# DeltaNet attention with a top-1 MoE on one core: the inverses' steps handed out by estimated VectorE time, norms and v moved later, blocks 12 to 15 routed as four

## The chip, the cores and the metric

One Trainium2 chip, of which one core is used. The metric is the device time of one execution in microseconds (us). The engines are TensorE (PE; its weight loads are listed apart as PEld), VectorE (DVE), ScalarE (ACT), GpSimd (POOL) and SyncE (SP), whose queue issues nearly all of the DMAs. Each engine works through its own queue in the order in which the program wrote it.

## The reference

Two layers. The first is a delta-rule recurrence over 768 tokens for 4 batches x 8 heads with head size 48; the second sends every one of the 3072 tokens (384 wide) to the one of 8 experts that its gate picks.

```python
# q, k, v: (4, 8, 768, 48); beta: (4, 8, 768); w1: (8, 384, 1024); w2: (8, 1024, 384)
k_n = k / (norm(k) + 1e-6)
for t in range(S):
    y[t] = q[t] @ state
    v_old = state^T k_n[t]
    state = state + beta[t] * outer(k_n[t], v[t] - v_old)
x = y as (3072, 384)
expert = argmax(x @ w_gate); gate = softmax value of that expert
out[token] = gate * (relu(x[token] @ w1[expert]) @ w2[expert])
```

## The kernel before, in words

**Blocks and steps.** The tokens are cut into 6 spans of 128 (`tb` from 0 to 5); a span of one batch with its 8 heads is a block, so there are 24 blocks, n = 4 tb + b. Inside a block the recurrence is solved in chunks of 32 tokens (`q` from 0 to 3) with the inverse of a triangular 32 x 32 matrix for each chunk and head. The main loop runs over steps t from 0 to 26. Step t works at once on chunk q of block t - q, for the four q's, in four groups of 32 partitions, so a block passes through four steps and a new one comes in at each.

**One step.** `residual(t)` (lines 441 to 470): TensorE adds up in `ks` what the state and the earlier chunks give, and VectorE subtracts it from v (line 470). `apply(t)` (473 to 485): TensorE multiplies the result with the inverses `wt` (line 478), ScalarE copies it to `u` (line 483). Line 478 can't start before line 470 has ended. Between the two, TensorE has the previous block's output transposes (`emit_x`, line 548, 8 matmuls) and in steps 1 to 4 a handful of filler matmuls (line 691, table `WD`). Then `finish(t - 3)` gives the outputs of the block that is complete, and `qpart` and `kpart` make the products for later blocks. At seven places of a step (`beside(t, i)`, i from 0 to 6) other work is written into the queues: entries of the list `off` that are due, steps of the inverses, steps of the routing (`fine`), pieces of the expert weights and of expert 0's first tokens (from step 20 on).

**The inverses.** Each span's inverses are made on VectorE alone, for all 32 (batch, head) pairs and 4 chunks at once. `prepare(tb)` computes the norms of k and scales the products (lines 320 to 362). `lanes(tb)` is the inverse: 16 columns, each with a multiplication (line 374) and a subtraction (line 385) on the two 16 x 16 halves, then `combine` for the lower left quarter (multiplications of line 395, additions of line 403), then one transpose into `wt` (line 418). That is 53 steps of the generator, of very different length. Span 0 is done ahead of the loop. Span tb is done in the steps 4 (tb - 1) to 4 tb - 1, and its transpose not before step 4 tb - 1. What is not yet done when step 4 tb begins is written there in one go. How many generator steps a place may take is a fixed count: `STEPS` (`STEPS0` in the first four steps); `prepare` uses the same count and gets three more of its own steps at each place.

**The mask.** `mask()` (line 303) is a GpSimd pass over the products that `qpart` left. It is made to wait for the last VectorE instruction that was noted ahead of the step ("beside the residual").

**Norms and v.** `norms` transposes the norms on VectorE (line 351) and writes them with four small DMAs of SP's queue into `nt_all` (line 354). `scale_v` (line 428) multiplies v with them, two steps' worth at once, in the odd steps; span tb's norms are first used in step 4 tb - 1. `load_v(tb, i)` loads chunk i of span tb's v into a ring of 8 (line 180) right behind `apply(t)` at t = 4 (tb - 1) + i - 1.

**Routing.** A finished block's rows go through `emit_x` into a row buffer, and `emit_slots` (lines 578 to 677) gives each token a slot in its expert's list: five small VectorE instructions (lines 589 to 606), counting matmuls (559), `pos` (625), `sli` (650), and one scatter per block from GpSimd's queue (658). Blocks 0 to 11 do this in fours, 12 to 15 in pairs, 16 on one by one. A set that has been started stands in the list `fine`; only its first member goes on. With fours, the scatters of the first pair are written one step after the set's start and those of the second pair one step later. The row buffers of blocks from 12 to 21 are two tiles of two rows, by turns; single blocks use half of one.

**Experts.** From step 20 on weights are loaded and split; expert 0's first tokens run in steps 23 to 26, and behind the loop the experts follow each other on TensorE.

Of the kernel before, what the change touches and what calls it, by code (L numbers as in the profile page):

```python
# [8 lines left out]
F32 = mybir.dt.float32  # L9
# [9 lines left out]
B, H, S, D = 4, 8, 768, 48  # L19
C = 128  # L20
NT = S // C
NB = C // 32
# [9 lines left out]
NN = NT * B  # L32
# [4 lines left out]
ROW = DM + E + 2  # L37
# [5 lines left out]
def deltanet_moe(ctx, tc, qT, kT, kr, v, beta, w_gate, w1, w2, out):  # L43
    nc = tc.nc
# [58 lines left out]
    HB = 16  # L103
# [1 line left out]
    LAG = NB - 1  # L105
    FILL = (0, 1, 4, 5, 6, 7, 2, 3)

    STEPS = (3, 3, 3, 3, 2, 2, 2)

    STEPS0 = (3, 3, 2, 2, 2, 2, 2)  # L110
    FINE = (3, 3, 3, 2, 2, 2, 2)
    W0 = 42
    WD = {1: 12, 2: 15, 3: 14, 4: 3}
    W1 = 8
    W4 = 12
    DM2 = 0
    DEF = 2
    AH = 3
# [12 lines left out]
    rp = ctx.enter_context(tc.tile_pool(name="rp", bufs=1, side="left"))  # L131
    lp_ = ctx.enter_context(ExitStack())
    ep_ = ctx.enter_context(ExitStack())
    lp = lp_.enter_context(tc.tile_pool(name="lp", bufs=1, side="left"))
    fp = ep_.enter_context(tc.tile_pool(name="fp", bufs=1, side="right"))
# [21 lines left out]
    nt_t = lp.tile([128, (NT * B + LAG) * H], F32, name="nt_all")  # L157
# [9 lines left out]
    tiles = {tb: {b: {} for b in range(B)} for tb in range(NT)}  # L167
# [150 lines left out]
    def prepare(tb):  # L318

        T = tiles[tb]  # L320
        if tb == 0:
            T["lg"] = fp.tile([128, LW], F32, name="lg0", tag="lg", bufs=2)
            tiles["mark"] = nc.vector.transpose(out=full(T["lg"]), in_=tiles["dg"]).ins
            yield
        lg = T["lg"]
        lw = T["lw"]
        ss, s0, r0 = (lp.tile([128, 32], F32, name=f"{n_}{tb}", tag=n_) for n_ in ("ss", "s0", "r0"))
        nc.vector.tensor_scalar(out=ss, in0=lg[:, 0:1024:33], scalar1=1e-36, scalar2=None, op0=ALU.max)
        for _ in range(6 if tb > 1 else 1):
            yield  # L330
        nc.scalar.activation(out=s0, in_=ss, func=AF.Sqrt)
        yield
        nc.vector.reciprocal(r0, s0)
        yield
        nc.vector.tensor_tensor(out=r0, in0=r0, in1=ss, op=ALU.mult)
        yield
        nc.vector.tensor_tensor(out=s0, in0=s0, in1=r0, op=ALU.add)
        yield
        nc.vector.tensor_scalar(out=s0, in0=s0, scalar1=0.5, scalar2=1e-6, op0=ALU.mult, op1=ALU.add)
        yield  # L340
        nc.vector.reciprocal(r0, s0)
        yield
        nc.vector.tensor_tensor(out=ss, in0=r0, in1=bl[:, tb, :], op=ALU.mult)
        yield
        nc.vector.tensor_tensor(out=lw.rearrange("p a b -> p (a b)")[:, 0:1024:33], in0=ss, in1=r0, op=ALU.mult)
        yield
        nc.vector.tensor_tensor(out=r0, in0=ss, in1=r0, op=ALU.mult)
        yield
        def norms():
            sn = lp.tile([128, 32], F32, name=f"sn{tb}", tag="sn")  # L350
            nc.vector.transpose(out=sn, in_=s0)
            for q in range(NB):
                p = slice(32 * q, 32 * q + 32)
                nc.sync.dma_start(out=nt_t[p, (B * tb + q) * H:(B * tb + q) * H + 32], in_=sn[p])
            yield

        nc.vector.tensor_tensor(out=blocks(lg), in0=blocks(lg), in1=r0.rearrange("p (f r) -> p f r", f=2).unsqueeze(3)
                                .broadcast_to([128, 2, HB, HB]), op=ALU.mult)
        T["scaled"] = True
        yield  # L360
        yield from norms()
        T["nt"] = True

    def lanes(tb):


        T = tiles[tb]
        lg, lw = full(T["lg"]), T["lw"]

        def product(nm, rows, cols, c):  # L370
            m, w = rows.stop - rows.start, cols.stop - cols.start
            x = fp.tile([128, 256 if rows.stop > 16 and c < 16 else 64], F32, name=f"{nm}{tb}_{c}", tag=nm, bufs=2)
            x = x[:, 0:m * w].rearrange("p (a b) -> p a b", a=m)
            noted(nc.vector.tensor_tensor(out=x, in0=lg[:, rows, c:c + 1].broadcast_to([128, m, w]),  # L374
                                          in1=lw[:, c:c + 1, cols].broadcast_to([128, m, w]), op=ALU.mult))
            return lw[:, rows, cols], x

        for c in range(HB):
            todo = [product("ta", slice(c + 1, 32), slice(0, c + 1), c)]
            if c < HB - 1:  # L380
                k = HB + c
                todo.append(product("tb", slice(k + 1, 32), slice(HB, k + 1), k))
            yield
            for y, x in todo:
                tiles["mark"] = noted(nc.vector.tensor_tensor(out=y, in0=y, in1=x, op=ALU.subtract))  # L385
            yield

        def combine(g):

            n, r0 = 4 * g + 4, HB + 4 * g  # L390
            x = fp.tile([128, 1024], F32, name=f"tc{tb}_{g}", tag="tc", bufs=2)
            x = x[:, 0:64 * n].rearrange("p (a j b) -> p a j b", a=4, j=n)
            for a0, a1 in ((0, 2), (2, 4)) if n > 8 else ((0, 4),):
                m = a1 - a0
                noted(nc.vector.tensor_tensor(out=x[:, a0:a1], in0=lw[:, r0 + a0:r0 + a1, HB:HB + n].unsqueeze(3)
                                              .broadcast_to([128, m, n, HB]),
                                              in1=lw[:, HB:HB + n, 0:HB].unsqueeze(1).broadcast_to([128, m, n, HB]),
                                              op=ALU.mult))
                yield
            while n > 1:  # L400
                h, k = n // 2, n - n // 2
                y = x[:, :, 0:h] if n > 2 else lw[:, r0:r0 + 4, 0:HB].unsqueeze(2)
                tiles["mark"] = noted(nc.vector.tensor_tensor(out=y, in0=x[:, :, 0:h], in1=x[:, :, k:n], op=ALU.add))
                n = k
                yield

        pair = [combine(g) for g in range(3, -1, -1)]
        while pair:
            for x in pair[0:2]:
                if next(x, 0) == 0:  # L410
                    pair.remove(x)
                else:
                    yield

        T["cols"] = True
        yield
        T["wt"] = lp.tile([128, BH, 32], F32, name=f"wt{tb}", tag="wt", bufs=2)
        tiles["mark"] = noted(nc.vector.transpose(out=T["wt"].rearrange("p h t -> p t h"), in_=lw))
        if tb + 2 < NT:
            clear_w(tb + 2)  # L420
        yield

    def scale_v(t):

# [62 lines left out]
    def finish(n):  # L487

        tb, b = n // B, n % B
# [5 lines left out]
        for p in range(NP):  # L495
            for a in range(2):
                x = slice(64 * (a ^ p % 2), 64 * (a ^ p % 2) + 64)
# [18 lines left out]
        for h in range(H):  # L516
            p, r = h // 2, 64 * (h % 2 ^ h // 2 % 2)
# [7 lines left out]
        j, m = n % w, min(w, 2)  # L525
# [1 line left out]
            tiles["rows"] = []  # L527
            tiles["rl"] = lp.tile([128, w, E], F32, name=f"rl{tb}_{b}", tag=f"rl{w}", bufs=2)
        if j % m == 0:
            pool, tag = (fp, "rowb") if j >= 2 else (rp, "row") if n < NN - 2 else (xq_[0], "row")  # L530
            t = pool.tile([128, 2 if n < NN - 2 else 1, ROW], F32, name=f"row{tb}_{b}", tag=tag, bufs=2)
            tiles["rows"].append(t[:, 0:m])
        xp = emit_x(n, yt, tiles["rows"][-1][:, j % m])
        yield
# [137 lines left out]
    def run(gen, steps=1):  # L672

        for _ in range(steps):
            if next(gen, tiles) is tiles:
                return False
        return True
# [283 lines left out]
    before = [(tb, prepare(tb)) for tb in range(1, NT)]  # L961
    W = None

    def inverses(steps, t, i=0):

        while steps > 0 and queue:
            tb, lane = queue[0]
            if t < B * (tb - 1) and "cols" not in tiles[tb - 1] or ("cols" in tiles[tb] and t < B * tb - 1):
                break
            if before and before[0][0] == tb:  # L970
                if (t, i) < READY.get(tb, (0, 0)):
                    break
                if run(before[0][1]):
                    steps -= 1
                else:
                    before.pop(0)
            elif run(lane):
                steps -= 1
            else:
                queue.pop(0)  # L980

    ahead, other = early(), rest()
    order = list(EO)
# [5 lines left out]
    def beside(t, i):  # L989

        tiles["t"], tiles["at"] = t, i
        due(t, i)
        inverses((STEPS0 if t < B else STEPS)[i], t, i)
        if before and (t, i) >= READY.get(before[0][0], (B * before[0][0] - B, 0)):
            if not run(before[0][1], 3):
                before.pop(0)
        for _ in range(FINE[i] if t < NN - B else 4):
            if fine and not run(fine[0]):
                fine.pop(0)
        for _ in range(WSL.count((t, i))):  # L1000
            run(W)
        for _ in range(ES.count((t, i))):
            ahead_step()

    fin = iter(())
    for t in range(NN + LAG):
# [31 lines left out]
        run(copies, 2)  # L1038
        for tb in range(1, NT):
            for i in range(NB):  # L1040
                if t == max(B * (tb - 1) + i - 1, 0):
                    load_v(tb, i)
        beside(t, 2)
        fin = finish(t - LAG) if t >= LAG else iter(())
# [280 lines left out]
```

## Time and profile before

| | us |
|---|---|
| median of 3 runs | 518.15 |
| the three runs | 517.04, 518.15, 521.36 |
| the profiled execution | 522.53 |
| its span, first to last instruction | 520.7 |
| TensorE busy | 484.5 |
| VectorE busy | 337.7 |
| ScalarE busy | 254.7 |
| GpSimd busy | 112.8 |

A stretch of the trace is given in us from the span's start. The steps of the loop take from 36 us to 284 us; the experts follow. "Idle before" is the time in which an engine did nothing before an instruction, with the instruction that ended the wait; "issue" stands for a wait that no semaphore of the trace explains. The granted clock is a share of TensorE's full speed: 1.00 is 2.4 GHz and 0.50 is 1.2 GHz; a value between them is a mean over a stretch with both.

### The profile page before, as it was taken

The page shows a single profiled execution, that of the slowest core. Times are in us where ns is not written, and L with a number is a line of the kernel's source. Part 1 is how long each engine was busy: PE and PEld are TensorE (multiplying, and loading weights), DVE is VectorE, ACT ScalarE, POOL GpSimd, SP SyncE. Part 2 cuts the span into 40 slices and gives each one's busy share as a digit, 9 for nine tenths or more (in the row PEclk, how much of TensorE's full clock was granted, in tenths as well). Part 3 has the DMA queues.
Part 4 walks back from the last instruction along what each step waited for, and adds up shares of the span by engine and source line. Part 5 has one row for each costly group of instructions (what it writes and reads, how often), then busy time and mean ns, then how long its engine had stood idle before and what let it go on. Part 6 is the DMA issues. An engine that isn't in the chain of part 4 may idle for free.

```text
span 520.7 us, 17340 instructions
## 1 busy us (share of the span) xinstructions
PE 484.5 (93%) x7286; PEld 434.8 (83%) x7291; DVE 337.7 (65%) x975; ACT 254.7 (49%) x539; POOL 112.8 (22%) x148
## 2 busy tenths in 40 slices
PE   7699899998998979999999999999999999999991
PEld 5656678887887868777889999999999999999991
DVE  2989959898689998465322976465756646565310
ACT  3413556674675645775343564444436444444210
POOL 6010121242242333323122001203030210303121
PEclk9999999997999989997999999999999999999997
DMA  6589747757554443762041595473847547481000
GB/s 197 121 194 256 188 140 192 220 157 183 145 156 107 136 121 107 244 198 91 18 102 68 163 239 157 121 183 115 203 124 164 160 134 161 141 197 36 13 18 27
DMA packets 74844, 74.14 MB, mean 142 GB/s; under 512 B 46649, under 2 KB 62506, under 8 KB 74764
## 3 DMA queue, kind: packets, MB, share of 16 engines
q1 hardware_dynamic: 71308, 63.45, 46.5%
q0 software_dynamic: 3456, 9.57, 5.1%
q8 instruction: 58, 0.95, 0.8%
q14 instruction: 22, 0.18, 0.1%
HBM read 54.25 MB, written 19.42 MB: 141 GB/s over the span
## 4 chain that ended last, share of the span: by engine, by line
PE 50%; issue 1%; ACT 1%; DMA 1%; SPq 1%; DVE 1%; POOL 1%; ACTq 0%; POOLq 0%
PE h L813 21%; PE y L824 18%; PE y L1131 4%; PE xp L548 1%; PE yp L518 1%; DMA w1r<-in_w_dram 1%; SPq L737 1%; PE ks L451 1%; PE ks L478 1%; PE pq L284 1%; PE ks L463 1%; PE xt L889 0%; POOL out_dram L827 0%; PE yp L498 0%; ACT pm L296 0%
## 5 line engine op out<-in xcount | busy, mean ns | idle before, releaser
L824 PE MATMUL y<-w2h,hx 128*128 128x384 f32 x352 | 93.2, 339 | 0.4 <-DVE hx L817 0.4
L827 POOL DMA_INDIRECT out_dram<-yo,idx x32 | 40.3, 1259 | 197.5 <-ACT yo L1126 113.0
L824 PEld LDWEIGHTS y<-w2h,hx 128*128 128x128 f32 x352 | 64.0, 188 | 1.2 <-DVE hx L817 1.1
L483 ACT COPY u<-ks 32x384 f32<-32x384 f32 x96 | 45.1, 469 | 33.7 <-PE ks L478 23.6
L813 PE MATMUL h<-xh,w1l 128*128 128x448 f32 x168 | 61.3, 365 | 0.0
L813 PE MATMUL h<-xh,w1h 128*128 128x448 f32 x168 | 61.2, 365 | 0.0
L813 PE MATMUL h<-xl,w1h 128*128 128x448 f32 x168 | 61.1, 363 | 0.0
L824 PE MATMUL y<-w2l,hx 128*128 128x384 f32 x176 | 59.4, 337 | 0.0
L698 DVE TENSOR_TENSOR w2l<-w2r,w2h 128x768 fp32r<-128x768 f32 x32 | 30.6, 957 | 40.6 <-ACT w2h L697 40.0
L817 DVE SCALAR_TENSOR_TENSOR hx<-h,hx 128x448 fp32r<-128x448 f32 (+1 forms) x64 | 37.5, 587 | 29.8 <-ACT hx L816 29.2
L816 ACT ACTIVATE hx<-h 128x448 fp32r<-128x448 f32 (+1 forms) x64 | 33.2, 518 | 44.8 <-PE h L813 44.8
L303 POOL TENSOR_SCALAR_AFFINE_SELECT pm<-pm 128x1024 f32<-128x1024 f32 x24 | 26.3, 1095 | 91.0 <-DVE tb L374 24.9
L1126 ACT ACTIVATE yo<-y,gt 128x384 f32<-128x384 f32 x22 | 12.8, 582 | 64.5 <-PE y L824 36.6
L451 PE MATMUL ks<-st,kt 112*32 112x96 f32 x768 | 43.5, 253 | 0.7 <-ACT st L512 0.5
L451 PEld LDWEIGHTS ks<-st,kt 112*32 112x32 f32 x768 | 32.4, 111 | 5.5 <-issue 1.9
L385 DVE TENSOR_TENSOR lw<-lw,ta 128x31 f32<-128x31 f32 (+7 forms) x96 | 36.6, 381 | 0.2
L284 PE MATMUL pg<-kt 48*128 48x128 f32 x384 | 31.7, 317 | 5.2 <-DMA kt<-in_kT_dram 4.2
L698 DVE TENSOR_TENSOR w1l<-w1r,w1h 128x1024 fp32r<-128x1024 f32 x24 | 29.4, 1225 | 9.0 <-ACT w1h L697 8.6
L478 PE MATMUL ks<-v_all,wt 32*32 32x48 f32 x1536 | 25.8, 206 | 10.1 <-DVE v_all L470 6.6
L284 PEld LDWEIGHTS pg<-kt 48*128 48x128 f32 x384 | 28.3, 222 | 8.3 <-issue 5.2
L658 POOL DMA_INDIRECT xg<-row,sli x22 | 22.6, 1028 | 58.0 <-ACT yt L522 20.4
L478 PEld LDWEIGHTS ks<-v_all,wt 32*32 32x32 f32 x1536 | 21.4, 107 | 16.4 <-DVE v_all L470 9.8
(166 smaller groups left out, 1038.3 us busy)
## 6 DMA issues: line engine op xcount, KB each, us to landing
w1r<-in_w_dram SPq DMA_DIRECT2D x24, 512.0 KB
w2r<-in_w_dram SPq DMA_DIRECT2D x32, 384.0 KB
xg<-zrow SPq DMA_DIRECT2D x14, 394.0 KB
kt<-in_kT_dram SPq DMA_DIRECT2D x24, 224.0 KB
qt<-in_qT_dram SPq DMA_DIRECT2D x24, 224.0 KB
xr<-xg SPq DMA_DIRECT2D x28, 168.0 KB
ku<-in_kr_dram SPq DMA_DIRECT2D x20, 192.0 KB
v_all<-in_v_dram SPq DMA_DIRECT2D x15, 192.0 KB
```

The source lines that it names most:

```text
L284: ins = nc.tensor.matmul(pg[a][:, p], lhsT=kt[r, p], rhs=xt[r, p], start=True, stop=True, tile_position=(64 * a, 0), skip_group_check=True)
L303: ins = nc.gpsimd.affine_select(out=pm, in_=pm, compare_op=ALU.is_gt, fill=0.0, base=0, pattern=[[0, H], [1, C]], channel_multiplier=-1)
L385: tiles["mark"] = noted(nc.vector.tensor_tensor(out=y, in0=y, in1=x, op=ALU.subtract))
L451: nc.tensor.matmul(ks[32 * q:32 * q + 32, 2 * p:2 * p + 2, :], lhsT=kt_t[n % KTL][0:RP, p, 32 * q:32 * q + 32], rhs=st_view(n % B, p), sta ...
L478: ins = nc.tensor.matmul(ks[r, h, :], lhsT=tiles[n // B]["wt"][r, n % B * H + h, :], rhs=vn[r, h, :], start=True, stop=True, tile_position ...
L483: nc.scalar.copy(out=uview(n)[r], in_=ks[r])
L698: nc.vector.tensor_tensor(out=lo, in0=src, in1=hi.bitcast(F32), op=ALU.subtract)
L813: nc.tensor.matmul(ps, lhsT=w[:, d, fs], rhs=x_[:, d], start=(n == 0), stop=(n == len(terms) - 1))
L816: nc.scalar.activation(out=hh, in_=ps, func=AF.Relu)
L817: nc.vector.scalar_tensor_tensor(out=hl, in0=ps, scalar=0.0, in1=hh.bitcast(F32), op0=ALU.max, op1=ALU.subtract)
L824: nc.tensor.matmul(ps, lhsT=h(f)[h_], rhs=w2[w][:, f, :], start=(n == 0), stop=(n == len(terms) - 1))
L827: nc.gpsimd.indirect_dma_start(out=out, out_offset=bass.IndirectOffsetOnAxis(ap=idx, axis=0), in_=yo, in_offset=None, bounds_check=N - 1, ...
```

## The change

Four edits.

1. **Shares.** A generator step of `lanes` now hands out an estimate of its VectorE time, `cost(n)` = 0.105 + 0.00098 n us for each instruction on n elements, and 1.92 for the transpose. A place of a step takes generator steps until its share (`SHARE`, 1.1 us at the first four places, 0.73 at the last three) is used up; what it went over is taken off at the next place. A step of `prepare` counts 0.3.
2. **Norms.** From span 2 on the four DMAs of the norms are put into `off` and written at step 4 (tb - 1) + 1, place 2.
3. **v.** From span 2 on `load_v(tb, i)` is written one step later, at t = 4 (tb - 1) + i.
4. **Blocks 12 to 15.** `W4` is 16, so they choose slots as one four. Their second row buffer is in another pool (one tile of two rows), and the single blocks 16 to 21 have two one-row tiles of their own (`rowc`).

```diff
-    STEPS = (3, 3, 3, 3, 2, 2, 2)
-    STEPS0 = (3, 3, 2, 2, 2, 2, 2)
+    SHARE = (1.1, 1.1, 1.1, 1.1, 0.73, 0.73, 0.73)
+    PREP = 0.3
-    W4 = 12
+    W4 = 16
...
+            if tb < 2:
+                spread()
+            else:
+                off.append(((B * (tb - 1) + 1, 2), spread))
+                off.sort(key=lambda x: x[0])
...
+    def cost(n):
+        return 0.105 + 0.00098 * n
...
         for c in range(HB):
             todo = [product("ta", slice(c + 1, 32), slice(0, c + 1), c)]
...
-            yield
-            for y, x in todo:
+            c_ = sum(x[2] for x in todo)
+            yield c_
+            for y, x, _ in todo:
                 tiles["mark"] = noted(nc.vector.tensor_tensor(out=y, in0=y, in1=x, op=ALU.subtract))
-            yield
+            yield c_
...
-        yield
+        yield cost(1850)
...
-            pool, tag = (fp, "rowb") if j >= 2 else (rp, "row") if n < NN - 2 else (xq_[0], "row")
-            t = pool.tile([128, 2 if n < NN - 2 else 1, ROW], F32, name=f"row{tb}_{b}", tag=tag, bufs=2)
+            pool, tag, k = ((fp if n < 12 else lp, "rowb", 2) if j >= 2 else (rp, "row", 2) if n < 16 else
+                            (lp, "rowc", 1) if n < NN - DEF else (xq_[0], "row", 1))
+            t = pool.tile([128, k, ROW], F32, name=f"row{tb}_{b}", tag=tag, bufs=1 if pool is lp and k > 1 else 2)
...
-    def inverses(steps, t, i=0):
-        while steps > 0 and queue:
+    def inverses(share, t, i=0):
+        left = min(tiles.get("left", 0), 0) + share
+        while left > 0 and queue:
...
                 if run(before[0][1]):
-                    steps -= 1
+                    left -= PREP
...
-            elif run(lane):
-                steps -= 1
             else:
-                queue.pop(0)
+                x = next(lane, None)
+                if x is None:
+                    queue.pop(0)
+                else:
+                    left -= x
+        tiles["left"] = left
...
-        inverses((STEPS0 if t < B else STEPS)[i], t, i)
+        inverses(SHARE[i], t, i)
...
-                if t == max(B * (tb - 1) + i - 1, 0):
+                if t == (max(i - 1, 0) if tb == 1 else B * (tb - 1) + i):
                     load_v(tb, i)
```

## Rows read from the trace of the kernel before

**Rows 1.** The page: TensorE's granted clock in 40 slices of the span

```profile
PEclk9999999997999989997999999999999999999997
```

**Rows 2.** Windows: stretch, length, busy us (instructions) by engine, granted clock, DMA share, GB/s

```profile
173.00:207.00 34.00, 30.23 (x877) 26.30 (x876) 31.55 (x118) 18.67 (x47) 12.70 (x15) 0.90 0.37 108
296.00:506.00 210.00, 209.99 (x1117) 202.13 (x1116) 119.22 (x198) 93.62 (x155) 36.38 (x28) 1.00 0.52 137
```

**Rows 3.** Waits of TensorE: engine, line, releaser: us in total, times, longest

```profile
PE ks L478 <- DVE v_all L470: 6.6, 8, 2.8
```

**Rows 4.** Timeline of TensorE, line 478: start, us, instructions [idle before, releaser]

```profile
71.72 0.37 PE L478 MATMUL ks<-v_all,wt 32*32 32x48 f32 x14 [1.14 <-issue]
...
96.01 0.58 PE L478 MATMUL ks<-v_all,wt 32*32 32x48 f32 x36 [0.37 <-DVE v_all L470]
...
120.70 0.78 PE L478 MATMUL ks<-v_all,wt 32*32 32x48 f32 x51 [0.51 <-DVE v_all L470]
122.73 0.53 PE L478 MATMUL ks<-v_all,wt 32*32 32x48 f32 x13 [1.25 <-issue]
...
158.04 0.66 PE L478 MATMUL ks<-v_all,wt 32*32 32x48 f32 x42 [0.81 <-DVE v_all L470]
...
166.61 0.58 PE L478 MATMUL ks<-v_all,wt 32*32 32x48 f32 x36 [0.79 <-DVE v_all L470]
...
191.54 1.50 PE L478 MATMUL ks<-v_all,wt 32*32 32x48 f32 x64 [2.77 <-DVE v_all L470]
```

**Rows 5.** Timeline of VectorE, steps 13 and 17: line 470 and what lies between

```profile
148.52 0.55 DVE L470 TENSOR_TENSOR v_all<-v_all,ks 128x384 f32<-128x384 f32 x1 [0.76 <-PE ks L463]
...
150.16 0.95 DVE L428 TENSOR_TENSOR v_all<-v_all,nt_all 128x768 f32<-128x768 f32 x1
...
157.44 0.55 DVE L470 TENSOR_TENSOR v_all<-v_all,ks 128x384 f32<-128x384 f32 x1
...
180.24 0.55 DVE L470 TENSOR_TENSOR v_all<-v_all,ks 128x384 f32<-128x384 f32 x1
...
190.93 0.55 DVE L470 TENSOR_TENSOR v_all<-v_all,ks 128x384 f32<-128x384 f32 x1
```

**Rows 6.** Timelines of GpSimd (first row) and VectorE (second row) at 191 us

```profile
191.18 1.09 POOL L303 TENSOR_SCALAR_AFFINE_SELECT pm<-pm 128x1024 f32<-128x1024 f32 x1 [5.74 <-DVE tb L374]
...
191.40 1.14 DVE L385 TENSOR_TENSOR lw<-lw,ta 128x252 f32<-128x252 f32 x1
```

**Rows 7.** Windows, columns as in rows 2: steps 10, 11, 18 and 19

```profile
122.73:131.88 9.15, 9.15 (x174) 7.83 (x173) 5.95 (x16) 5.28 (x12) 1.45 (x2) 0.63 0.41 93
132.88:139.88 7.00, 7.00 (x235) 6.17 (x234) 5.00 (x14) 5.97 (x17) 1.66 (x2) 1.00 0.47 121
...
191.54:199.88 8.34, 8.34 (x209) 7.32 (x209) 8.04 (x23) 4.11 (x10) 3.50 (x5) 0.63 0.39 118
200.88:206.69 5.81, 5.81 (x215) 5.10 (x214) 5.26 (x15) 4.69 (x12) 0.58 (x3) 1.00 0.26 79
```

**Rows 8.** Timeline of VectorE, step 17: first and last of a pair's five

```profile
182.71 0.17 DVE L589 TENSOR_REDUCE mx<-rl 128x2 f32<-128x16 f32 x1
...
183.54 0.17 DVE L606 TENSOR_TENSOR ohb<-oh,m 128x16 bf16<-128x16 f32 x1
```

**Rows 9.** DMA view, 120.3 to 121.6 us: instruction queue, packets, MB, share of 16 engines

```profile
q8 instruction: 1, 0.02, 4.2%
```

**Rows 10.** Waits of SP's queue, 68 to 210 us

```profile
SPq L180 <- PE ks L478: 13.2, 11, 3.3
...
SPq L354 <- DVE lw L385: 10.4, 4, 3.6
```

**Rows 11.** Timeline of ScalarE, step 21

```profile
216.13 0.48 ACT L549 COPY row<-xp 128x384 f32<-128x384 f32 x1 [2.24 <-DMA xg<-row,sli]
```

**Rows 12.** Timeline of GpSimd, step 22

```profile
223.72 0.99 POOL L658 DMA_INDIRECT xg<-row,sli  x1 [6.50 <-ACT yt L522]
```

**Rows 13.** Timeline of TensorE, step 2, behind the fillers

```profile
52.43 0.88 PE L478 MATMUL ks<-v_all,wt 32*32 32x48 f32 x48 [0.58 <-DVE v_all L470]
```

More of the change, by code (lines that the diff above doesn't have):

```diff
@@ L351, in norms, with spread @@
             nc.vector.transpose(out=sn, in_=s0)
-            for q in range(NB):
-                p = slice(32 * q, 32 * q + 32)
-                nc.sync.dma_start(out=nt_t[p, (B * tb + q) * H:(B * tb + q) * H + 32], in_=sn[p])
+            def spread():
+                for q in range(NB):
+                    p = slice(32 * q, 32 * q + 32)
+                    nc.sync.dma_start(out=nt_t[p, (B * tb + q) * H:(B * tb + q) * H + 32], in_=sn[p])
+            if tb < 2:
[3 more added lines that the diff above has]
+                off.sort(key=lambda x: x[0])
             yield
@@ L375, in product @@
                                           in1=lw[:, c:c + 1, cols].broadcast_to([128, m, w]), op=ALU.mult))
-            return lw[:, rows, cols], x
+            return lw[:, rows, cols], x, cost(m * w)
         for c in range(HB):
@@ L398, in combine @@
                                               op=ALU.mult))
-                yield
+                yield cost(m * n * HB)
             while n > 1:
@@ L404, in combine @@
                 n = k
-                yield
+                yield cost(4 * h * HB)
         pair = [combine(g) for g in range(3, -1, -1)]
@@ L409, in lanes @@
             for x in pair[0:2]:
-                if next(x, 0) == 0:
+                c_ = next(x, 0)
+                if c_ == 0:
                     pair.remove(x)
                 else:
-                    yield
+                    yield c_
         T["cols"] = True
-        yield
+        yield 0
         T["wt"] = lp.tile([128, BH, 32], F32, name=f"wt{tb}", tag="wt", bufs=2)
@@ L420, in lanes @@
             clear_w(tb + 2)
-        yield
+        yield cost(1850)
     def scale_v(t):
```

## The prediction, made before the changed kernel was built or run

> **What bounds the kernel now.** Begin with the second half, because there is more of it. From 296 to 506 us TensorE is busy for 209.99 of 210.00 us at a granted clock of 1.00 [rows 2]; nothing of the change touches that work, so whatever the loop saves or loses moves the end by as much. Next comes the loop. In span 5's steps, 173 to 207 us, TensorE is busy 30.23 of 34.00 us and VectorE 31.55, and the clock is 0.90 [rows 2]: the two engines are nearly matched, and the clock is not full. The clock's slices show three dips in the loop [rows 1]. The waits say what TensorE stands still for: line 478 for line 470, the subtraction on VectorE, 6.6 us over eight places [rows 3]; no other wait of TensorE on an engine comes near it. The timeline gives the places [rows 4]: 0.37 in step 7, 0.51 in step 10, 0.81 and 0.79 in steps 14 and 15, 2.77 in step 18. VectorE isn't slow with the subtraction (0.55 us); it comes late to it, because the inverses' instructions stand ahead in its queue. In step 13 it has 8.92 us of work from one line 470 (148.52) to the next (157.44), in step 17 10.69 us (180.24 to 190.93) [rows 5].
>
> What does TensorE need? In step 11 its part from line 478 to the end of the next residual takes 7.00 us at a clock of 1.00, in step 19 5.81 us, and about 1.0 us lies from there to the next line 478 (131.88 to 132.88) [rows 7]. So a step is 8.0 us about steps 10 to 13 and 6.8 to 7.1 us in steps 15 to 19. VectorE's 8.9 and 10.7 are over that.
>
> Lateness costs twice more. First, the mask. It is tied to VectorE's last instruction ahead of the step, so on a late step GpSimd starts it (191.18, 1.09 us) when line 470 starts, and VectorE's next instruction, 0.42 us long elsewhere, lasts 1.14 [rows 6]: 0.7 us more VectorE work on every late step. Second, the clock. After the stops of steps 10 and 18 the mean clock is 0.63 in the rest of the step, so part of it runs at 1.2 GHz in place of 2.4 [rows 7]. Step 18 then takes 8.34 us where step 19 takes 5.81: 2.5 us. In step 10, 9.15 us and the 0.78 us ahead of its second stop stand against 7.00: 2.9 us [rows 4, 7].
>
> **Shares.** I count the generator's 53 steps with the change's own cost function, for spans 2 to 5, step by step of the loop. Before: 2.9, 8.4, 7.4 and 3.4 us in the four steps that an inverse has; after: 3.3, 7.0, 6.4 and 5.4 (22.1 both times; nothing is left for the end). How good is that unit? Step 13 holds 8.4 of it in 8.92 - 0.55 (line 470) - 0.95 (scaling) = 7.4 us [rows 5], so a unit is 0.9 us here. VectorE's work after the change is then:
> second step, 8.92 - 1.4 x 0.9 = 7.7 us;
> third, 8.57 (line 478 at 158.04 and 166.61, VectorE late at both [rows 4]) - 0.7 for the mask - 0.9 = 7.0;
> fourth, 5.4 x 0.9 and line 470, scaling, and a routing set of 1.2 = 7.6 to 7.9.
> In steps 4 to 15 TensorE's 8.0 covers them, and the waits of steps 7, 10, 14 and 15 go: 0.37 + 0.51 + 0.81 + 0.79 = 2.5 us.
>
> In span 5 it doesn't. TensorE's step is 6.8 to 7.1 us there, and step 15 hands on 7.9 - 7.1 = 0.8 us of lateness. Step 17 is 10.69 - 0.7 - 1.3 = 8.7 and, without the pair's routing (below), 7.6; step 18 7.0; step 19 8.2. Carried from step to step, with 0.7 for the mask on each late step and 0.4 us of lateness hidden behind line 548, this gives TensorE waits of 0.5, 0.2, 1.3, 0.6 and 2.1 us in steps 16 to 20: 4.7 us where there were 2.77. The transpose that moved one place back in step 19 is the reason for the last one.
>
> In steps 0 to 3 VectorE has no gap and its sum stays the same, but step 0 gets 1.3 units more, 1.1 us, ahead of line 470 of step 1. TensorE's fillers then run later and step 2's wait of 0.58 us [rows 13] absorbs about half: +0.5 us.
>
> **Norms and v.** SP's queue waits 13.2 us for line 478 (v's ring) and 10.4 us for the transpose of the norms [rows 10]; both vanish. What is queued behind them on SP, the loads of q and k for later blocks, leaves earlier, but nothing waits for these: the only releaser of TensorE's big waits is line 470 [rows 3]. The v of a span is first multiplied two or three steps after the new issue, over 14 us, the norms two steps after theirs. I take nothing, with bounds of 0.5 us either way for traffic that meets other traffic.
>
> **Blocks 12 to 15 as four.** One of two sets goes. A set is five instructions from 182.71 to 183.71 us [rows 8] and two more, 1.2 us, and the one that goes was in step 17, the worst. That is in the sum above. Scatters of blocks 12 and 13 leave GpSimd two steps later and those of 14 and 15 one. Behind them in `fine` stand the single blocks: block 17's scatter comes to stand behind the mask of step 22 instead of ahead of it [rows 12]. Expert 0's first load waits for it, so the price lies between nothing and a mask, 1.09 us; the mask will then start earlier than it did, so I take 0.2. The own buffers take away the wait of step 21, where ScalarE's copy into a row stood 2.24 us until an older scatter had landed [rows 11]. Its matmuls would have held it 1.0 us and its usual pause some 0.5 in any case: bounds 0 and 2.24, I take -0.7.
>
> **The clock.** Neither fall is the change's own; they follow the stops. Step 10 keeps a stop of 1.25 us that waits for no engine [rows 4]; the nearest row is the stop of 1.14 us in step 4, also without a releaser, after which no dip shows [rows 1, 4]. So I take the fall of step 10 as gone, -2.9. Step 18's wait shrinks to 1.3, step 20's grows to 2.1, and of the rows that is nearest to 2.77, which had a fall. So one fall of 2.5 stays and only changes its place.
>
> Is the 1.25 us stop really none of VectorE's? In that stretch the instruction queue moved a packet [rows 9], which is why I leave the stop in. The Trainium skill, Runtime: NRT & Kernel Launch, Instruction fetch mechanics, says that crossing a block of instructions is "mostly hidden". By that page the stop would belong to the wait and go with it, 1.25 us more; no row here settles it.
>
> **The sum.** Against the profiled 522.53 us: -2.5 (steps 4 to 15); 4.7 + 2.5 - 2.77 - 2.5 = +1.9 (span 5); +0.5 (start); +0.2 - 0.7 (routing); -2.9 (clock in step 10). That is -3.5, or 519.0. The median, 518.15, lies 4.4 us under the profiled execution, the size of one and a half falls; so the usual execution probably has fewer of them, and I count only half of the 2.9: -2.05 from the median, **516.1 us**.
>
> **Rivals.**
> The clock stays full through span 5, since none of its new waits reaches 2.77. Then 2.5 us more come back: 513.6. For it: 0.81, 0.79 and 1.14 passed without a dip. Against it: 2.1 us is far over these.
> The stop of step 10 goes with the wait, and its fall wholly: 1.25 + 1.45 more, 513.4. For it: the stop follows 0.78 us behind the late start. Against it: rows 9.
> Slower: span 5 is overfilled. VectorE's work in steps 15 to 19 is 38 us against TensorE's 35. If the wait at step 18 stays above 2 us the clock falls there and again behind step 20's, and with step 10's fall also back that is 2.5 + 1.45 on the forecast, 520.1, over the 518.15 of before. The point that decides is a subtraction about 2 us behind the residual at both steps.
> It doesn't do what it says: if a unit differs much between products and combinations, step 4k + 1 stays as full as it was. The units of 0.9 against a fit of 1.0 speak against it. 518 us.
>
> **How the numbers follow.** Forecast 0.45, full clock in span 5 0.22, stop gone 0.1, overfilled 0.15, no effect 0.08. The range reaches from 511.0 (two of the faster cases together) to 520.5 (overfilled, with the unknown 0.4). A difference of 1% (5.2 us) is about what a measurement of this kernel can tell from no change. Under 513.0 lie half of the two faster cases and a little more: 0.2. Over 523.3 is overfilled with a further fall: 0.05. The rest, 0.75, is within 1%.
>
> **What will show it.** Line 470 should start right behind the residual in steps 7, 10, 14 and 15, and late in 16 to 20; the instruction behind it should be long only on late steps; VectorE's work of a step should be under 8 us for steps 5 to 18; the SP waits for line 478 and for the norms should be gone; ScalarE shouldn't wait in step 21. The forecast is wrong if the granted clock falls elsewhere, for its price is as large as that of all waits together.

## The result, and the profile after

The changed kernel takes 522.75 us (median of 20 runs, 518.83 to 524.98) where the kernel before takes 519.44 (20 runs): a ratio of 1.0055 [1.0036, 1.0075], 0.55% slower, some 2.9 us (the medians lie 3.3 apart). The forecast was 516.1, faster by 2.05, with 520.5 as the range's upper end. The sign is wrong. In all that follows the ratios leave out runs over 1.5% above the fastest of their kernel and the medians don't: that is 5 of 12 runs of `only_loads`, 3 of 12 of `only_shares`, and the profiled executions of `only_fours` and `only_loads`, which are read for places and not for times.

The profiled execution of the changed kernel took 521.16 us, its span 519.5. That is less than the 522.53 of the execution shown of before, so the two traces laid side by side would show a gain; the medians do not. What the traces can be read for is places: which steps became shorter, and which longer. First the page's clock, which answers to [rows 1]:

```profile
PEclk8699999999999999888998999999999999999996
```

The dips of steps 10 and 18 are not there. Three slices with an 8 stand between 208 and 247 us, where the kernel before had one dip, in step 23, and another 8 stands behind the loop (273 to 286 us). The windows of the changed kernel (columns as in [rows 2]: span 5, the second half, then step 10, 18, 20, 21 and 22, each from one start of line 482 to the next; line 482 is the subtraction, line 470 before, and line 490 is TensorE's line 478 before):

```profile
173.00:207.00 34.00, 30.01 (x939) 25.45 (x938) 30.04 (x100) 20.93 (x53) 11.78 (x15) 1.00 0.47 144
296.00:506.00 210.00, 210.00 (x1120) 202.14 (x1119) 116.86 (x194) 93.38 (x155) 37.15 (x29) 1.00 0.52 135
117.92:125.63 7.71, 7.71 (x233) 6.80 (x234) 7.06 (x21) 5.57 (x13) 1.14 (x3) 1.00 0.77 168
183.47:191.15 7.68, 7.01 (x220) 5.98 (x218) 7.61 (x22) 4.87 (x12) 1.45 (x2) 1.00 0.37 101
199.63:207.28 7.65, 6.58 (x210) 5.36 (x211) 4.02 (x11) 4.97 (x11) 4.89 (x6) 1.00 0.83 275
207.28:219.12 11.84, 8.49 (x223) 6.67 (x222) 5.39 (x16) 6.66 (x15) 5.36 (x6) 0.90 0.74 214
219.12:228.09 8.97, 8.97 (x221) 7.86 (x222) 3.63 (x11) 6.26 (x14) 0.37 (x2) 0.75 0.38 114
```

The second half is the same. Span 5 runs at a clock of 1.00 where [rows 2] had 0.90. The last two rows are the find: step 21 takes 11.84 us and step 22 8.97. The same two steps of the kernel before:

```profile
206.77:214.48 7.71, 7.37 (x220) 6.23 (x221) 3.12 (x12) 5.62 (x13) 3.14 (x4) 1.00 0.90 305
214.48:222.94 8.46, 7.34 (x220) 6.21 (x221) 5.15 (x13) 6.56 (x14) 2.45 (x3) 1.00 0.54 155
222.94:230.39 7.45, 7.31 (x221) 6.37 (x222) 4.40 (x13) 6.13 (x14) 2.46 (x3) 1.00 0.66 196
```

Step 21 starts at 207.28 us, 7.2 ahead of the 214.48 of before; step 23 starts at 228.09, only 2.3 ahead of 230.39. So 4.9 us are lost in two steps (20.81 - 15.91). Behind them step 23 gives 1.0 us back: it takes 10.76 us against 11.72, with a fall of the clock in both. Another 1.6 us go between the last subtraction and the next expert's first matmul (19.11 us against 17.55): the clock falls there from about 278 to 281 us, and a fall stands at that place in five of the nine traces with shares (below) and in none of the three without. Why is open; `both_pairs_at_once` has that fall too, so it is not what sets it apart from the changed kernel. What TensorE waited for in the two steps, in its waits (as [rows 3]):

```profile
PE ks L490 <- DVE v_all L482: 6.2, 7, 1.4
...
PE sb L572 <- DVE pos L638: 1.9, 1, 1.9
```

The wait for the subtraction is in total nearly as long as it was, though no longer 2.8 at once. The second row is new: line 572 is the counting of the routing, three matmuls on 8 columns for a single block. The timeline of TensorE in step 21 (start, us, instructions, idle before and its releaser):

```profile
210.57 0.18 PE L572 MATMUL sb<-ohb,utri 128*128 128x8 bf16 x1
...
211.91 1.04 PE L530 MATMUL yp<-pm,u 128*48 128x128 f32 x15
214.85 0.17 PE L572 MATMUL sb<-ohb,utri 128*128 128x8 bf16 x1 [1.90 <-DVE pos L638]
214.88 0.17 PE L572 MATMUL sb<-ohb,ltri 128*128 128x8 bf16 x1
214.90 0.17 PE L572 MATMUL sb<-ohb,ones 128*128 128x8 bf16 x1
215.00 0.86 PE L463 MATMUL ks<-st,kt 112*32 112x96 f32 x24
...
217.06 0.28 PE L475 MATMUL ks<-u,gg 128*32 128x48 f32 x1 [0.44 <-issue]
...
218.97 2.04 PE L561 MATMUL xp<-esel,yt 128*128 128x104 f32 x8
```

and that of VectorE beside it:

```profile
213.50 1.23 DVE L711 TENSOR_TENSOR w1l<-w1r,w1h 128x1024 fp32r<-128x1024 f32 x1 [1.62 <-ACT w1h L710]
214.64 0.16 DVE L638 TENSOR_TENSOR pos<-sb,ohb 128x8 f32<-128x8 f32 x1
...
219.12 0.55 DVE L482 TENSOR_TENSOR v_all<-v_all,ks 128x384 f32<-128x384 f32 x1 [3.65 <-PE ks L475]
```

Read it backwards. Line 482 of step 22 (219.12) waits 3.65 us for the residual. The residual, lines 463 and 475, starts at 215.00, because the count of block 17 stands ahead of it in TensorE's queue and waits 1.90 us. That count adds to the sums in PSUM (`sb`) that line 638 multiplies for block 16, so it may not start before line 638 has read them. Line 638 (214.64) stands behind line 711, a weight split that itself waited 1.62 us for ScalarE. Behind the wait the clock falls: the residual's matmuls come with pauses, line 561 takes 2.04 us for what is 1.14 in other steps, and step 22 has a mean clock of 0.75.

Before, the two counts lay a whole step apart, at 210.26 in step 20 and 217.89 in step 21 (timeline of TensorE, kernel before):

```profile
210.26 0.18 PE L559 MATMUL sb<-ohb,utri 128*128 128x8 bf16 x1
...
217.89 0.18 PE L559 MATMUL sb<-ohb,utri 128*128 128x8 bf16 x1
```

What moved them is the order list `fine`, from which a block is taken only when the one ahead is done. The four 12 to 15 issues its second pair of scatters in step 21 and holds the list until then; block 16 counts right behind it, and block 17 in the same step.

The waits at line 490 in the loop (TensorE, steps 1, 14, 16, 18, 19 and 20), which answer to [rows 4] and [rows 13]:

```profile
44.66 0.87 PE L490 MATMUL ks<-v_all,wt 32*32 32x48 f32 x32 [1.01 <-DVE v_all L482]
...
152.08 0.88 PE L490 MATMUL ks<-v_all,wt 32*32 32x48 f32 x64 [0.56 <-DVE v_all L482]
...
168.23 1.11 PE L490 MATMUL ks<-v_all,wt 32*32 32x48 f32 x64 [1.36 <-DVE v_all L482]
...
184.07 0.88 PE L490 MATMUL ks<-v_all,wt 32*32 32x48 f32 x64 [0.26 <-DVE v_all L482]
...
191.75 0.88 PE L490 MATMUL ks<-v_all,wt 32*32 32x48 f32 x64 [1.01 <-DVE v_all L482]
...
200.21 0.88 PE L490 MATMUL ks<-v_all,wt 32*32 32x48 f32 x64 [1.36 <-DVE v_all L482]
```

Steps 7, 10 and 15 have none left; span 5 has 3.99 us in smaller pieces (1.36 + 0.26 + 1.01 + 1.36).

### The profile page after: what moved, and what is told of

Its sections match the earlier page's. It is cut to its first block, busy times and chain, and to the rows that moved or that the text cites. A ratio compares the mean times of both kernels' runs of the same rounds, so it can differ in the third digit from the quotient of the medians.

```text
span 519.5 us, 17333 instructions
## 1 busy us (share of the span) xinstructions
PE 483.4 (93%) x7290; PEld 432.3 (83%) x7290; DVE 336.7 (65%) x968; ACT 255.4 (49%) x541; POOL 113.3 (22%) x148
## 4 chain that ended last, share of the span: by engine, by line
PE 73%; DVE 12%; DMA 4%; issue 4%; ACT 3%; SPq 1%; POOL 1%; DVEq 0%; ACTq 0%; POOLq 0%
PE h L826 21%; PE y L837 18%; PE y L1148 4%; PE ks L463 4%; PE pg L283 4%; PE wm L704 3%; PE xp L561 3%; PE pq L283 3%; PE ks L490 3%; DVE lw L396 3%; PE yp L530 3%; PE ks L475 2%; DMA kt<-in_kT_dram 2%; DVE ta L384 2%; PE yp L510 2%
## 5 line engine op out<-in xcount | busy, mean ns | idle before, releaser
L463 PE MATMUL ks<-st,kt 112*32 112x96 f32 x768 | 45.6, 250 | 1.4 <-issue 1.2
L711 DVE TENSOR_TENSOR w1l<-w1r,w1h 128x1024 fp32r<-128x1024 f32 x24 | 30.5, 1271 | 9.9 <-ACT w1h L710 9.4
L396 DVE TENSOR_TENSOR lw<-lw,ta 128x31 f32<-128x31 f32 (+7 forms) x96 | 34.4, 359 | 0.2
L384 DVE TENSOR_TENSOR ta<-lg,lw 128x31 f32<-128x31 f32 (+7 forms) x96 | 33.9, 354 | 0.0
L826 PEld LDWEIGHTS h<-xh,w1l 128*128 128x128 f32 x168 | 31.6, 188 | 2.6
```

The lines of the kernel that those rows point to most:

```text
L463: nc.tensor.matmul(ks[32 * q:32 * q + 32, 2 * p:2 * p + 2, :], lhsT=kt_t[n % KTL][0:RP, p, 32 * q:32 * q + 32], rhs=st_view(n % B, p), sta ...
L711: nc.vector.tensor_tensor(out=lo, in0=src, in1=hi.bitcast(F32), op=ALU.subtract)
L826: nc.tensor.matmul(ps, lhsT=w[:, d, fs], rhs=x_[:, d], start=(n == 0), stop=(n == len(terms) - 1))
```

## The experiments

**The theories.** Theory 1: the order of the routing costs the time, because TensorE is blocked in step 21. Theory 2: the inverses' shares overfill span 5, and its waits and falls of the clock cost the time. Theory 3: the later loads of the norms and of v do. Each kernel ran in 12 runs (`light_start` in 6) beside the kernel before on the same chip; `split_later` to `only_shares` ran on one chip, `both_pairs_at_once` to `changed_again` on another, the last two on a third.

The table has, from windows of each profiled execution, the start of step 20, the lengths of steps 21 and 22 (from one subtraction to the next) and the mean granted clock of steps 10, 18, 21 and 22.

| kernel | ratio to before | step 20 at | 21 | 22 | clock 10, 18, 21, 22 |
|---|---|---|---|---|---|
| before | 1 | 206.77 | 8.46 | 7.45 | 0.71 0.63 1.00 1.00 |
| changed | 1.0055 [1.0036, 1.0075] | 199.63 | 11.84 | 8.97 | 1.00 1.00 0.90 0.75 |
| split_later | 0.9994 [0.9956, 1.0031] | 204.82 | 8.37 | 12.22 | 0.84 0.64 1.00 0.58 |
| pairs_again | 0.9962 [0.9928, 0.9996] | 205.75 | 8.36 | 7.87 | 0.84 0.64 1.00 1.00 |
| only_fours | 1.0028 [0.9992, 1.0065] | 208.00 | 10.96 | 7.69 | 0.72 1.00 0.86 0.98 |
| only_shares | 0.9970 [0.9928, 1.0012] | 204.53 | 9.09 | 7.45 | 0.84 0.64 1.00 1.00 |
| both_pairs_at_once | 0.9927 [0.9894, 0.9960] | 202.35 | 8.46 | 7.45 | 1.00 0.64 1.00 1.00 |
| old_loads | 1.0054 [1.0018, 1.0091] | 204.50 | 10.88 | 8.89 | 1.00 1.00 0.84 1.00 |
| only_loads | 0.9974 [0.9930, 1.0017] | 208.12 | 7.87 | 7.45 | 1.00 1.00 1.00 1.00 |
| changed_again | 1.0016 [0.9976, 1.0056] | 203.48 | 10.90 | 8.59 | 1.00 0.64 0.81 0.85 |
| light_start | 0.9899 [0.9855, 0.9943] | 202.53 | 8.31 | 7.45 | 1.00 1.00 1.00 1.00 |
| light_start_more_early | 0.9960 [0.9925, 0.9996] | 204.66 | 10.39 | 7.44 | 1.00 1.00 0.84 1.00 |

**split_later.** The changed kernel; the fourth weight split is issued one place later, so that line 638 of block 16 doesn't stand behind it.

```diff
-    WSL = ((20, 1), (20, 3), (21, 1), (21, 3), (22, 1), (22, 3), (23, 1), (23, 3))
+    WSL = ((20, 1), (20, 3), (21, 1), (21, 4), (22, 1), (22, 3), (23, 1), (23, 3))
```

> The changed kernel with one entry of the weights' table moved: the piece that was split at step 21, place 3, is split at place 4, so that in VectorE's queue block 16's multiplication of the slots (pos) stands ahead of the split and no longer behind it. Theory 1 (the loss is made in step 21, where block 17's counting on TensorE waits for pos of block 16, which stands behind a split that waits for ScalarE; 1.9 us of waiting, then a fall of the clock, some 4 to 5 us in all): ratio to the kernel before 0.995 to 0.999, that is 517 to 519 us where the changed kernel has 522.75; TensorE waits under 0.3 us ahead of the counting in step 21. Theory 2 (the shares overfill span 5, steps 16 to 20): no change against the changed kernel, about 1.0055. Theory 3 (norms and v later meet other transfers): no change either, about 1.0055.

521.6 us. The count of block 17 no longer waits, though it is still in step 21 (timeline of TensorE, `split_later`):

```profile
215.74 0.18 PE L572 MATMUL sb<-ohb,utri 128*128 128x8 bf16 x1
...
217.50 0.18 PE L572 MATMUL sb<-ohb,utri 128*128 128x8 bf16 x1
...
221.43 0.37 PE L490 MATMUL ks<-v_all,wt 32*32 32x48 f32 x14 [0.40 <-DVE v_all L482]
222.81 1.27 PE L490 MATMUL ks<-v_all,wt 32*32 32x48 f32 x50 [1.02 <-issue]
```

Step 21 is back at 8.37 us. But the split now stands ahead of the subtraction of step 22, which comes 0.40 us late; a stop of 1.02 follows, and the clock falls to a mean of 0.58: 12.22 us for that step. So the wait does come from the split ahead of line 638. A gain in time is not shown: the ratio misses the 0.995 to 0.999 expected, and it stands 0.6% under that of the changed kernel's first measurement but only 0.2% under `changed_again`'s (below), with overlapping intervals. This execution gives the gain back one step later.

**pairs_again.** The changed kernel with blocks 12 to 15 in pairs.

```diff
-    W4 = 16
+    W4 = 12
```

> The changed kernel with W4 back at 12: blocks 12 to 15 choose slots in pairs, all else as changed (shares, norms and v later, the single blocks' own row buffers). Theory 1: block 17's counting is back at place 3 of step 21 and the wait is gone; ratio to the kernel before 0.996 to 1.000, with VectorE 1.2 us later in span 5 than in the changed kernel, from the pair's routing in step 17. Theory 2: span 5 gets fuller still, ratio 1.007 to 1.010. Theory 3: as the changed kernel, 1.0055.

518.98 us, 0.9962: with the shares and the new loads, but without the four, the kernel is faster than before, as theory 1 expected. TensorE has no wait at the counting in steps 21 and 22, which take 16.23 us together.

**only_fours.** The kernel before with W4 = 16 and the row buffers of the change.

```diff
-    W4 = 12
+    W4 = 16
-            pool, tag = (fp, "rowb") if j >= 2 else (rp, "row") if n < NN - 2 else (xq_[0], "row")
+            pool, tag, k = ((fp if n < 12 else lp, "rowb", 2) if j >= 2 else (rp, "row", 2) if n < 16 else
+                            (lp, "rowc", 1) if n < NN - DEF else (xq_[0], "row", 1))
```

> The kernel before with only the routing edit: blocks 12 to 15 as four, the second buffer and the single blocks' buffers as in the change; steps of the inverses by count, norms and v as before. Theory 1: the wait of step 21 and the fall behind it are there; ratio 1.006 to 1.010 (3 to 5 us slower). Theory 2: step 17 loses a pair's routing, so ratio 0.996 to 1.000. Theory 3: the same, 0.996 to 1.000.

523.01 us, 1.0028. Its interval just holds 1, and the loss is smaller than the 1.006 to 1.010 that theory 1 expected. The wait is in its trace all the same, without any of the shares (waits of TensorE, `only_fours`; line 560 is the count there):

```profile
PE sb L560 <- DVE pos L626: 2.7, 1, 2.7
```

**only_shares.** The kernel before with the shares in place of the steps (SHARE, PREP, `cost` and the new `inverses`, as in the diff of the change).

> The kernel before with only the inverses' steps by shares; routing, buffers, norms and v as before. Theory 1: the waits for line 470 in steps 7, 10, 14 and 15 shrink or go, span 5 stays late; ratio 0.994 to 0.999. Theory 2: 1.004 to 1.008, with waits of together over 6 us in steps 16 to 20. Theory 3: 0.994 to 0.999, as theory 1.

520.38 us, 0.9970. Theory 2 asked for a loss of 0.4% or more here; the interval ends at 0.12%. TensorE stands still in the span for 1.37 us in step 16, 0.82 in step 17, 0.40 in step 18 and 0.75 in step 20, and for 1.64 us without a releaser just ahead of step 18: together 4.98, not over 6. The fall in step 18 (0.64) is there too, but the kernel before has that as well, with its wait of 2.77.

**both_pairs_at_once.** The changed kernel; the four 12 to 15 issues all four scatters in one step, so it leaves the list in step 20.

```diff
-                while tiles["t"] == t1 or tiles["at"] < (2 if w == 2 else 3):
+                while (j == 0 or n0 < 12) and tiles["t"] == t1 or tiles["at"] < (2 if w == 2 else 3):
```

> The changed kernel with one difference: blocks 12 to 15 still choose as four, but their two pairs of scatters are issued in the same step, so the generator of the four ends a step earlier and the counting of blocks 16 and 17 should go back to their earlier places. Theory 1 (TensorE is blocked in step 21, because the counting of block 17 waits there for the slots of block 16): the wait of TensorE at line 572 in step 21, 1.90 us, is gone, step 21 takes 8 to 9 us in place of 11.84, and the time is 3 to 5 us under the changed kernel's. Theory 2 (the inverses' shares overfill span 5, and its waits and clock falls make the loss): no difference from the changed kernel, within 1 us. Theory 3 (the later loads of norms and v cost the time): no difference either.

518.07 us, 0.9927, where the changed kernel beside it on the same chip has 1.0016: 0.9% apart, 4.6 us, and the intervals do not overlap. The four still choose together, the shares are the same, the splits are at their places. Only the list moved, and with it the scatters of blocks 14 and 15, a step earlier (timeline of TensorE, then windows of steps 21 and 22, `both_pairs_at_once`):

```profile
205.44 0.18 PE L572 MATMUL sb<-ohb,utri 128*128 128x8 bf16 x1
...
213.25 0.18 PE L572 MATMUL sb<-ohb,utri 128*128 128x8 bf16 x1
214.18 0.17 PE L572 MATMUL sb<-ohb,ltri 128*128 128x8 bf16 x1 [0.75 <-DVE ohb L619]
```

```profile
209.81:218.27 8.46, 7.13 (x220) 6.12 (x221) 6.67 (x13) 6.57 (x14) 3.43 (x5) 1.00 0.68 225
218.27:225.72 7.45, 7.29 (x221) 6.34 (x222) 3.76 (x11) 6.15 (x14) 2.46 (x3) 1.00 0.74 216
```

The counts lie a step apart again, no count waits for line 638, and the two steps take 15.91 us, what they took before the change and 3.6 less than in `changed_again` (19.49). A wait of 0.75 us for the choice of block 17 is left.

**old_loads and only_loads.** The first is the changed kernel with the old places of the norms' writes (no `spread` put off) and of v's loads, the second the kernel before with the new ones. The line of v's loads, as `only_loads` changes it and `old_loads` turns it back:

```diff
-                if t == max(B * (tb - 1) + i - 1, 0):
+                if t == (max(i - 1, 0) if tb == 1 else B * (tb - 1) + i):
```

> The changed kernel with the norms written and v loaded at their earlier places; shares and fours stay. Theory 3 (the later loads cost the time): 2 us or more under the changed kernel. Theories 1 and 2: the same time as the changed kernel, within 1 us; SP's waits for the ring of v and for the norms are back, over 10 us each, and nobody waits for what stands behind them.

> The kernel before with the norms' and v's move alone. Theory 3: 2 us or more over the kernel before. Theories 1 and 2: no difference from the kernel before, within 1 us; SP's two waits are gone.

523.94 us, 1.0054, and 523.31, 0.9974. Neither shows the loss of 2 us by the later loads that theory 3 asked for: by the ratios both differences from their own base (1.0016 and 1) point to a small gain, inside the intervals. By its median `only_loads` stands above the kernel before (523.31 against 521.96), so even the sign of so small an effect stays open. SP's waits are back in `old_loads` (waits of SP's queue, 60 to 215 us):

```profile
SPq L179 <- PE ks L483: 12.2, 9, 2.7
...
SPq L354 <- DVE lw L389: 9.5, 3, 4.6
```

In the changed kernel they have not vanished so much as moved: there the same queue waits for line 510 (same view, changed kernel):

```profile
SPq L179 <- PE yp L510: 27.3, 12, 5.9
```

Whether any of `old_loads`' 0.4% over `changed_again` comes from its waits isn't shown. `old_loads` has theory 1's wait as well, 2.7 us in step 21.

**changed_again.** The changed kernel itself, on the second chip.

> The changed kernel itself, for comparison on this chip with the three beside it: 2 to 4 us over the kernel before by all theories. Theory 1: step 21 takes over 10 us, with the wait at line 572, in this execution too. Theory 2: the waits behind line 482 in steps 16 to 20 come to 4 us or more, with a fall of the clock in the steps that follow.

522.58 us, 1.0016: less over the kernel before than the 2 to 4 us expected, on a chip where that took 521.96. The interval holds 1, and the loss that the first measurement shows is not confirmed by this one. Its trace answers to theory 1 (2.7 us at line 572 and 10.90 us for step 21) and has the waits of theory 2 too, 1.36, 0.82, 1.68 and 0.75 in steps 16, 17, 18 and 20, with a clock of 0.64 in step 18.

**light_start.** `both_pairs_at_once` with smaller shares at two places of steps 0 to 3.

```diff
-        inverses(SHARE[i], t, i)
+        inverses(0.73 if t < B and i > 1 else SHARE[i], t, i)
```

> The changed kernel with both pairs of scatters in one step, as the run before it, and in steps 0 to 3 a share of 0.73 in place of 1.1 at the two stations 2 and 3 of a step. The prediction priced the heavier step 0 at 0.5 us. If that is right, TensorE's wait behind line 482 in step 1 (1.01 to 1.49 us) falls under 0.6 and the loop reaches step 4 some 0.5 us earlier: 0.9918 of the kernel before, where the run with both pairs at once stood at 0.9927. The rival: the fillers take it up, and nothing changes. Theory 1 again: no wait at line 572 for the slots in step 21.

517.02 us, 0.9899, the lowest ratio here, and ahead of both kernels. Step 1's wait is (timeline of TensorE, `light_start`)

```profile
44.93 0.87 PE L490 MATMUL ks<-v_all,wt 32*32 32x48 f32 x32 [0.22 <-DVE v_all L482]
```

where the run with both pairs at once had 1.23. From the first subtraction to that of step 4 it takes 30.79 us against 31.52: 0.7 us. The ratios are of different chips and their intervals overlap, so the size rests on the traces.

**light_start_more_early.** The same with shares 1.12 times as large in steps 4 to 15.

> The same, and in steps 4 to 15 shares 1.12 times as large, so that an inverse is done earlier in its last step and step 15 hands less work on to step 16. If the wait of 1.36 us at line 490 in step 16 comes from VectorE's lateness handed on by step 15, it shrinks below 0.7 and the time falls by 0.5 to 1 us more; if it comes from the work of step 16 itself (the preparation of the next inverse), it stays at 1.36 and the second steps of each inverse wait instead, for no gain or a loss of up to 1 us.

519.52 us, 0.9960: no gain, some loss. The wait of step 16 is gone, which fits lateness that step 15 had handed on; step 15 itself now waits 0.67. But another stop, in step 9, grew to 2.04 us, with no releaser, and that step took 12.97 us, with a clock of 0.74, where `light_start` took 8.21. Step 21 took 10.39, with 0.83 us of wait for the choice of block 17, a stop of 0.88 and a clock of 0.84 (timeline of TensorE, `light_start_more_early`):

```profile
114.52 0.61 PE L490 MATMUL ks<-v_all,wt 32*32 32x48 f32 x36 [2.04 <-issue]
```

Whether the larger shares cause these is open.

## Why the prediction was wrong

**The step that failed** is the routing term: "block 17's scatter comes to stand behind the mask of step 22 instead of ahead of it [rows 12] ... so the price lies between nothing and a mask, 1.09 us; ... I take 0.2". It followed the list `fine` to GpSimd's queue and stopped there. A block in that list issues counting matmuls on TensorE and line 638 on VectorE as well, and these move in the list together with its scatter. The +0.2 measured 4.9 us in the profiled execution and 0.9%, 4.6 us, in the direct comparison of `changed_again` with `both_pairs_at_once`, of which their traces show 3.6 in these two steps. From the forecast, -2.05, to the first measurement, +2.9, it is 5.0 us. Of the 4.9, 3.4 are step 21's (11.84 against 8.46: 1.90 of wait, the rest pauses and a clock of 0.90) and 1.5 step 22's (8.97 against 7.45 at 0.75). What the fall alone costs was not tried apart; the prediction's own sign of being wrong, a fall of the clock elsewhere, is there in steps 21 and 22. Nor did GpSimd's queue do what was forecast: block 17's scatter left at 217.04, still ahead of the mask of 218.02, and earlier than the 223.72 of before [rows 12].

None of the rivals held it either. The one on the slower side was an overfilled span 5, and `only_shares`, with span 5's standstills about as large as forecast, is not shown slower.

**The other steps**, one by one:

- Steps 4 to 15: -2.5 forecast. Of the waits of steps 7, 10, 14 and 15 only 0.56 us in step 14 are left, nearly as forecast. The time shows less of it. In the four traces with shares whose clock is full there (`changed`, `both_pairs_at_once`, `old_loads`, `changed_again`) these steps take 100.47 to 103.03 us, 101.5 in the mean, and in `only_loads`, which has the old steps and a full clock, 102.11. So the waits went, but the 2.5 us that they were priced at is not shown; where the rest went is open.
- VectorE's work per step, forecast for the second, third and fourth step of an inverse at 7.7, 7.0 and 7.6 to 7.9 us: 7.71, 7.26 and 7.82 in steps 5 to 7. Right. Under 8 us it doesn't stay: 8.34 in step 13, 8.28 in step 15, 8.22 in step 17, so VectorE is late from step 13 on and not only from step 16.
- Span 5: 4.7 us of waits forecast at 0.5, 0.2, 1.3, 0.6 and 2.1. Measured 3.99 in the changed kernel's trace and 4.61 in `changed_again`. The sum of the waits is right, the places are not: 1.36 comes already in step 16, and step 20 has 1.36 or 0.75. The term made of them, +1.9, did not come: steps 16 to 20 take 39.65 us in the changed kernel's trace and 40.87 in `changed_again`, 41.68 before.
- The clock in step 18: the fall was to move to step 20. It didn't. In five of the nine traces with shares step 18 has 0.64, behind waits of 1.6 to 1.9 us or a pair of stops, and step 20 has no fall in any of these five. In the other four (`changed`, `old_loads`, `light_start`, `light_start_more_early`) step 18 has 1.00; `light_start` waited 1.69 us there. Which way it goes stays open.
- The clock in step 10: the fall was to go, and half of 2.9 was counted. The two traces with the stop's fall in full are `before` and `only_fours` (0.71 and 0.72). With shares six of nine traces have 1.00 and three 0.84; in two of the six a fall stands beside it, in step 11 (0.84, `light_start`) or 9 (0.74, `light_start_more_early`). About right in size; but `only_loads`, without shares, has 1.00 too, so that the shares took the fall away isn't shown.
- The stop of step 10 itself: the forecast left it in. `changed_again` shows it, 0.97 us behind 50 matmuls of line 490 with no wait ahead of it (123.52), as the kernel before had 1.25 behind 51 [rows 4]. So it doesn't go with the wait, and that rival falls, though in the changed kernel's own trace step 10 has no such stop. By the Trainium skill, Runtime: NRT & Kernel Launch, Instruction fetch mechanics, crossing a block of instructions is "mostly hidden"; if these stops are such crossings, which no run here isolates, the trace doesn't agree.
- Steps 0 to 3: +0.5 forecast. With a full clock they take 31.22 to 31.52 us in three traces, 31.17 before, and `light_start` gives 0.7 back: right in kind, and if anything smaller. What the forecast put at nothing is a fall there. Four of the seven traces with the full shares have one in step 0 or 1 (a clock of 0.67 to 0.80) and take 31.79 to 33.98 us; none of the three without shares has one, and neither light start. That the shares cause these falls was not tried apart.
- Norms and v: nothing forecast, with 0.5 either way. `only_loads` and `old_loads` agree within their intervals, which are wider than that, some 2 us. That SP's waits vanish was wrong: those for line 478 and for the norms went, and others took their place.
- ScalarE's wait in step 21 for an older scatter [rows 11]: gone. The row copy of that step (208.18) waits for TensorE's line 561 alone.

All of the forecast but the routing can be weighed at once. `both_pairs_at_once` keeps the shares, the loads and the choice as four, and takes away the block of step 21: 0.9927 [0.9894, 0.9960], where the forecast was 516.1 of 518.15, 0.9960, the interval's slower end. And `only_shares` measured -1.6 us (0.3% of 521) where the terms of the shares make -2.5 + 1.9 + 0.5 - 1.45 = -1.55; its interval reaches from a gain of 3.8 us to a loss of 0.6. That the two agree is partly luck: the +1.9 counts step 17 without the pair's routing, which `only_shares` still has, and by the traces steps 4 to 15 gave less than forecast and span 5 took less.

Of TensorE's order the Trainium skill, Perfetto Trace Analysis, Tensor Engine Instruction (MATMUL, LD_WEIGHTS), says that its queue has a limited reorder, which can take weight loads ahead of matmuls in flight. The trace agrees as far as it goes: no matmul of the residual passed the waiting count, and the 24 of line 463 began at 215.00, 0.15 us behind it.

## What to carry to other kernels

When a step leaves an ordered list later, follow everything behind it in the list on every engine, the smallest matmuls first: a count of three matmuls of 0.17 us that waits for a VectorE result holds up the whole of TensorE's queue, and the result stands behind whatever VectorE does there. Put two uses of one accumulator in the same step only if nothing long stands ahead of the read between them. And read a pair of traces for places, not for their difference: here the two profiled executions stood 1.4 us apart with the wrong sign, and falls of the clock come and go between executions: the changed kernel itself had 1.00 in steps 1 and 18 in one execution, and 0.74 and 0.64 in another.

## What was not expected of the hardware

A fall of the clock can follow a wait of 1.90 us in step 21 (a mean of 0.75 in the step behind it) and not follow waits of 1.36 us in steps 16 and 20 of the same execution; in step 18 a wait of 1.68 was followed by 0.64 (`changed_again`) and one of 1.69 by 1.00 (`light_start`), so the length of the wait alone doesn't decide.

Stops of TensorE without a releaser come back at the same instruction in kernels that differ: behind 50 or 51 matmuls of line 490 (478 before) in step 10 (0.97 us in `changed_again`, 1.25 before), and in step 9 ahead of the last 36, with 0.95 us in `changed_again` and 2.04 in `light_start_more_early`.
